# Block-sparse attention with a channel mixer: six sampled block numbers per register load, masked by VectorE, and a new order from the planner

## The chip, the cores and the metric

One Trainium2 chip, one core. The metric is the device time of one execution in microseconds. The kernel before takes 584.38 us, the median of three runs (582.27 to 584.39).

## The reference, cut to what matters

```python
def _attn_ref(q, k, v, sampled_blocks):          # 4 batches, 8 heads, 768 positions, 64 wide
    block, n_blocks = 32, 24
    scores = q @ k^T / sqrt(64)
    mask = neighbouring blocks | first or last block, as row or as column
    for qb in range(n_blocks):
        for kb in sampled_blocks[qb]:            # 3 numbers per query block
            mask[rows of qb, columns of kb] = True
    return softmax(where(mask, scores, -1e9)) @ v

def _moe_ref(x, mu_k, mu_r, w_k, w_v, w_r):      # x: heads side by side, 512 wide
    x_prev = x shifted by one position
    xk, xr = mu_k * x + (1 - mu_k) * x_prev, mu_r * x + (1 - mu_r) * x_prev
    v = relu(xk @ w_k) ** 2 @ w_v                # 512 -> 1024 -> 512
    return sigmoid(xr @ w_r) * v
```

The mixer's weights come as 64-bit numbers, and the kernel converts them. The numbers in `sampled_blocks` are known only at run time.

## The kernel before, in words

The four batches are worked in two pairs (`pr`), 0 and 1. Attention is cut into units. Two wide units, one per pair, hold the first and the last query block, which see all keys. The other 22 query blocks of a pair make 11 near units of two neighbouring query blocks each (`UNITS`, `load_near`, `near_unit`), so there are 22 near units in all. A near unit needs its queries (`q`), eight key blocks for each of its query blocks and the values that belong to them.

Keys lie in one buffer, `KR0`; one load (`kd`) brings the neighbouring blocks and six fetches (`kt`, line 520) bring the sampled ones, three per query block. Since `KR_BUFS` is 1, the keys of a unit can be loaded only when the scores of the unit before are done. Values lie in six buffers `VR`, used in pairs: for each query block one load (`vn`, line 533) and three fetches of sampled blocks (`vt`, line 540).

From the seventh unit on (`CARRY`) the probabilities `p` are transposed in blocks by VectorE (`tb`, line 607), and SyncE moves the pieces back to `p` with four transfers (line 613); the products with the values (line 664) wait for these. The earlier units transpose on TensorE (line 584).

Nearly all transfers are issued by SyncE, from one queue, in the order in which the program has them. A sampled fetch needs a register that holds the block's number. VectorE packs the three numbers of a query block into one word (`pack`, lines 327 to 332). `sampled_block` loads that word into a register, once per query block (a load, a check of its bounds), and then takes a number out of it with a shift and a mask, which are register operations on SyncE ahead of each fetch. The registers of the first pair of batches are used again for the second.

When a batch pair has a tile of 128 positions finished, the mixer works on it: `gate` (`r`, line 862), `hidden` (`h`, line 888 or 904) and `values` (`v`, line 922). Its matmuls stand between those of the attention units, and the last four tiles, taken two at a time, stand at the end.

The order of all operations is set by a planner (`Plan.order`): each operation is added with an engine, a duration, a rank and the buffers it uses, and the planner simulates the engines and places them. The ranks come from tables of numbers (`UNIT_AT`, `KEYS_AT`, `VALUES_AT`, `TILE_AT`, `WEIGHT_AT`, `CONVERT_AT`). The durations that SyncE's operations are planned with are constants: 450 ns for an issue and for each of the four moves of `p`, 680 for a sampled fetch, 640 for the loads of a query block's word. They set the order only; what an operation takes on the chip doesn't depend on them.

Of the kernel before, what the change touches and what calls it, by code (L numbers as in the profile page):

```python
# [9 lines left out]
F32 = mybir.dt.float32  # L10
# [261 lines left out]
def block_sparse_attention_channel_mix(  # L272
# [15 lines left out]
    def fixed(shape, dtype, name):  # L288
        return Fixed(cp.tile(shape, dtype, name=name))
# [13 lines left out]
    packed = fixed([1, NB], I32, "packed")  # L303
# [10 lines left out]
    def mask_setup():  # L314
# [3 lines left out]
        word = buf([P, 2 * NB], F32, "x1", 1, "word")  # L318
# [178 lines left out]
    def load_near(pr, m, i):  # L497
# [27 lines left out]
        for j in range(PAIR):  # L525
# [9 lines left out]
            def gather(w=w, j=j, more=more):  # L535
# [3 lines left out]
                for i in range(NRAND):  # L539
                    nc.sync.dma_start(to[:, i], vt[bass.ds(sampled_block(n + j, i) + pr * NB, 1)].rearrange("o k b x -> (o k) (b x)"))  # L540
# [3 lines left out]
            plan.add(SP, NRAND * FETCH + ISSUE * more, values_at + 0.01 * j, gather, reads=[(packed,)],  # L544
# [59 lines left out]
    def carry(p, keys, name, rank):  # L604
# [10 lines left out]
        plan.add(SP, QB * ISSUE, rank + 0.05, away, reads=[(turned,), (p, *keys)], writes=[(p, *keys)], size=QB * wire(180000, 1024), parts=QB)  # L615
# [416 lines left out]
ISSUE, FETCH, FIND = 450, 680, 640  # L1032
# [20 lines left out]
TWICE = -83.1032  # L1053
# [4 lines left out]
O_MAX, O_EXP, O_TR, O_PV, O_END = 5.0819, 5.7451, 5.4616, 26.0916, 5.9388  # L1058
W_MAX, W_EXP, W_TR, W_PV = -123.0937, 6.5274, 5.6492, -188.6436
O_MIX, O_SQ, O_SQ1 = -0.0059, 100.3872, -9.1324  # L1060
NEAR, STAY, STORE = 78.2721, -9.6694, 0.0
SECOND = 0.4468
UNIT_AT = [
    -10.1623, 39.0943, 41.5342, 48.1709, 60.9108, 87.2056, 142.7255, 143.5689, 209.2752,
    223.9713, 253.2747, 259.3255, 264.4496, 276.0797, 315.2623, 326.072, 346.1908, 362.7343,
    379.7602, 404.9611, 414.6551, 432.6396, 446.0631, 552.0929, 566.7713,
]
KEYS_AT = [
    -10.1028, -44.6072, 30.887, -99.6782, 55.0175, 65.6048, 75.2198, 80.1323, 92.2395,
    97.8406, 117.16, 69.934, 137.2921, 148.3066, 186.9807, 192.5333, 262.4631, 209.2797,  # L1070
    315.8413, 265.1049, 367.6119, 371.1823, 392.2787, 340.6908,
]
VALUES_AT = [
    14.772, -16.2249, 42.8975, 81.9301, -30.9551, 104.2473, 116.8682, -135.6146, 80.6142,
    175.7208, 188.4774, 102.1683, 198.1179, 228.8766, -7.598, -553.0218, -325.0968, -355.2257,
    -606.1065, -400.3997, -436.2148, -1.5444, 196.7775, 208.1251,
]
# [14 lines left out]
T_RATE = 1.5576
# [58 lines left out]
```

## Time and profile before

| | us |
|---|---|
| median of three runs | 584.38 |
| profiled execution, its own time | 583.11 |
| its span, first to last instruction | 581.3 |
| TensorE (PE) busy in the span | 524.7 |
| VectorE (DVE), ScalarE (ACT), GpSimd (POOL) busy | 301.3, 289.5, 298.1 |

Busy times are sums over the instructions of an engine, so idle time is the span less the busy time. The mean granted TensorE clock was 0.977 of full speed. SyncE's instructions are not counted as busy time; what it did is read from the timeline of its queue (SPq). A time in the trace is counted from the span's start.

### The profile page before, as it was taken

What the parts mean: (1) busy time and instruction counts of PE and PEld (TensorE: products, weight loads), DVE (VectorE), ACT (ScalarE), POOL (GpSimd) and SP (SyncE); (2) the same over time, 40 slices, a digit from 0 to 9 for tenths busy, and PEclk for the clock granted to TensorE, in tenths of its full rate; (3) what the DMA queues carried; (4) which work ended last, traced back from release to release, by engine and by line L of the source; (5) the groups of instructions that cost most, each with busy time, mean ns of one, the idle gap of its engine ahead of it and who ended that gap; (6) DMA issues with size and microseconds to landing.
All of it is one profiled execution on the core that took longest, in us unless ns stands there. A gap on an engine that the chain in (4) does not pass through costs nothing.

```text
span 581.3 us, 17991 instructions
## 1 busy us (share of the span) xinstructions
PE 524.7 (90%) x6883; PEld 413.0 (71%) x6883; DVE 301.3 (52%) x787; ACT 289.5 (50%) x707; POOL 298.1 (51%) x368
## 2 busy tenths in 40 slices
PE   7877756899987999799999998987999999999997
PEld 3535434687766778489788876775788788888886
DVE  2587797859954454625554644653565542231201
ACT  3665675548634444715547447355457363514420
POOL 0144548668644607417655257146548269656820
PEclk9999797999998999899999999998999999999999
DMA  8999998888777888977748788866878750010001
GB/s 309 379 359 347 326 329 282 270 290 304 233 226 225 248 266 246 273 237 216 222 126 262 229 266 238 271 180 214 248 224 263 229 136 1 1 54 19 1 19 54
DMA packets 72376, 125.29 MB, mean 216 GB/s; under 512 B 11553, under 2 KB 47010, under 8 KB 72290
## 3 DMA queue, kind: packets, MB, share of 16 engines
q1 hardware_dynamic: 72002, 123.75, 66.9%
q8 instruction: 54, 0.88, 0.6%
q10 hardware_dynamic: 288, 0.39, 0.2%
q14 instruction: 32, 0.26, 0.1%
HBM read 100.77 MB, written 6.55 MB: 185 GB/s over the span
## 4 chain that ended last, share of the span: by engine, by line
PE 56%; DMA 18%; SPq 11%; ACT 5%; issue 4%; DVE 4%; POOL 1%; DVEq 0%; ACTq 0%; POOLq 0%
PE v L922 18%; PE s L628 5%; DMA p<-tb 5%; PE o L664 5%; DMA k_ring<-kw 4%; SPq L540 4%; PE r_1p L862 3%; PE r_0p L862 3%; PE h_1p L888 3%; ACT p L573 3%; DMA KR<-kt 2%; DMA VR<-vt 2%; SPq L520 2%; SPq L613 2%; PE h_3p L888 2%
## 5 line engine op out<-in xcount | busy, mean ns | idle before, releaser
L922 PE MATMUL v<-wv,k 128*128 128x512 f32 (+1 forms) x600 | 141.2, 389 | 0.7 <-ACT z L869 0.7
L922 PEld LDWEIGHTS v<-wv,k 128*128 128x128 f32 x600 | 108.2, 189 | 27.3 <-issue 2.9
L564 DVE CUSTOM_DVE_ANT_1 p<-s,near_mask 128x256 f32<-128x256 f32 x176 | 91.1, 628 | 56.7 <-PE s L628 28.5
L573 ACT ACTIVATE p<-p,nm 128x256 f32<-128x256 f32 x176 | 87.6, 499 | 65.7 <-DVE nm L564 58.3
L628 PE MATMUL s<-KR,q 64*32 64x256 f32 x1408 | 52.3, 412 | 11.2 <-DMA KR<-kt 8.0
L607 DVE STREAM_TRANSPOSE tb<-p 128x1024 f32<-128x1024 f32 x32 | 39.8, 1243 | 29.1 <-DMA p<-tb 23.8
L838 POOL TENSOR_TENSOR xr<-xr_1f,xr 128x256 fp32r<-128x256 f32 x24 | 18.2, 758 | 63.3 <-ACT xr L836 63.0
L628 PEld LDWEIGHTS s<-KR,q 64*32 64x32 f32 x1408 | 27.8, 113 | 28.5 <-issue 13.2
L930 DVE SCALAR_TENSOR_TENSOR z<-v,z 128x512 f32<-128x512 f32 (+1 forms) x25 | 16.7, 668 | 57.7 <-PE v L922 41.4
L664 PE MATMUL o<-VR,p 128*32 128x64 f32 x2048 | 36.6, 220 | 8.4 <-DMA p<-tb 5.4
L664 PEld LDWEIGHTS o<-VR,p 128*32 128x32 f32 x2048 | 31.4, 110 | 15.3 <-DMA p<-tb 8.2
L829 DVE SCALAR_TENSOR_TENSOR xr_0f<-xr_0d,mk,xt 128x128 f32<-128x128 f32 x48 | 20.5, 468 | 33.3 <-POOL xr L838 23.7
L825 POOL TENSOR_TENSOR xr_1d<-xt 128x128 f32<-128x128 f32 x48 | 19.3, 420 | 29.1 <-DVE xr_0f L829 17.3
L573 ACT ACTIVATION_READ_ACCUMULATOR p<-p,nm 128x1 f32 x176 | 33.0, 187 | 0.0
L862 PE MATMUL r_1p<-wr,xr 128*128 128x512 f32 x120 | 30.4, 400 | 0.9 <-ACT h_3k L874 0.9
L862 PE MATMUL r_0p<-wr,xr 128*128 128x512 f32 x120 | 31.2, 402 | 0.0
L417 POOL TENSOR_TENSOR wf<-wf,early 128x512 f32<-128x512 f32 x8 | 10.4, 1295 | 40.4 <-DVE wf L406 31.2
L829 DVE SCALAR_TENSOR_TENSOR xr_1f<-xr_1d,mk,xt 128x128 f32<-128x128 f32 x48 | 17.9, 413 | 22.6 <-POOL xr L838 19.8
L888 PE MATMUL h_1p<-mixed,wk 128*128 128x256 f32 x192 | 26.3, 293 | 3.2 <-issue 3.2
L825 POOL TENSOR_TENSOR xr_0d<-xt 128x128 f32<-128x128 f32 x48 | 20.2, 441 | 16.8 <-DVE xr_0f L829 7.2
L564 DVE DVE_READ_ACCUMULATOR2_ANT nm<- 128x1 f32 x176 | 28.0, 159 | 0.0
L888 PEld LDWEIGHTS h_1p<-mixed,wk 128*128 128x128 f32 x192 | 25.0, 200 | 4.1 <-issue 3.3
(172 smaller groups left out, 1035.8 us busy)
## 6 DMA issues: line engine op xcount, KB each, us to landing
VR<-vn SPq DMA_DIRECT2D x44, 512.0 KB, 4.8
VR<-vt SPq DMA_DIRECT2D x138, 128.0 KB, 3.7
KR<-kt SPq DMA_DIRECT2D x132, 128.0 KB, 3.6
p<-tb SPq DMA_DIRECT2D x128, 128.0 KB, 2.8
KR<-kd SPq DMA_DIRECT2D x22, 512.0 KB, 5.0
v_ring<-vw SPq DMA_DIRECT2D x16, 384.0 KB, 6.0
out<-z SPq DMA_DIRECT2D x23, 256.0 KB, 2.8
q<-qn SPq DMA_DIRECT2D x22, 256.0 KB, 3.8
```

What stands on the lines that cost most here:

```text
L540: nc.sync.dma_start(to[:, i], vt[bass.ds(sampled_block(n + j, i) + pr * NB, 1)].rearrange("o k b x -> (o k) (b x)"))
L564: nc.vector.tensor_tensor_reduce(out=dealt(p.ap[:, cs]), in0=cut(view()), in1=by, scale=-SCALE, scalar=3e38 if first is None else nm.ap[:, ...
L573: plan.add(ACT, 378 + 0.83 * (cs.stop - cs.start), rank, lambda: nc.scalar.activation(p.ap[:, cs], p.ap[:, cs], AF.Exp, bias=nm.ap[:, col ...
L607: plan.add(DVE, 1250, rank, lambda: nc.vector.transpose(out=turned.ap.rearrange("p (k y c) -> p k y c", k=QB, c=BLK), in_=p.ap.rearrange(" ...
L628: nc.tensor.matmul(s.ap[ROWS[j], row, a * 256 : (a + 1) * 256].rearrange("p (x g a) -> p g a x" if carried else "p (x a g) -> p g a x", g= ...
L664: nc.tensor.matmul(o.ap[ROWS[j], h * D : (h + 1) * D], held[gi][1](i, g, j), VR[values[j % PAIR][g]].ap[:, j // PAIR, h * D : (h + 1) * D] ...
L825: sub.tensor_tensor(out=part(d.ap), in0=x.ap[:, two, c, 1 : 1 + TT], in1=x.ap[:, two, c, 0:TT], op=ALU.subtract)
L829: nc.vector.scalar_tensor_tensor(out=part(f.ap[:, i, :]), in0=part(d.ap), scalar=mk.ap[:, which, c : c + 1], in1=x.ap[:, two, c, 0:TT], op ...
L838: plan.add(POOL, 80 + 2.4 * MIX * tw, rank + O_MIX, lambda f=f, cs=cs: nc.gpsimd.tensor_tensor(out=dst.ap[:, 1, cs], in0=f.ap, in1=dst.ap[ ...
L862: nc.tensor.matmul(pr.ap[:, 0:512], xr.ap[:, a, c, :], wr.ap[:, w, c, :], start=(c == 0 and m == 0), stop=(c == CC - 1 and m == 2))
L888: nc.tensor.matmul(ph.ap[:, ff * PAIR * TT : (ff + 1) * PAIR * TT], wk.ap[:, w, c, f * P : (f + 1) * P], xk.ap[:, a, c, :], start=(c == 0 ...
L922: nc.tensor.matmul(pv.ap[:, 0:width], hid[f][2](a), wv.ap[:, w, f, cs], start=(f == 0 and m == 0), stop=(f == FC - 1 and m == 2))
```

## The change

The word is no longer packed. VectorE masks all 72 numbers with one operation to their five low bits, and `packed` holds 72 numbers. SyncE loads the six numbers of a near unit with one load into six registers, without a check of bounds, once for each unit of both pairs; no shift and no mask stands ahead of a fetch. The planner is given other durations for SyncE's operations, and all its tables are new.

```diff
-    packed = fixed([1, NB], I32, "packed")
+    packed = fixed([1, NB * NRAND], I32, "packed")
...
         def pack():
-            v = nc.vector
-            n = number.ap.rearrange("o (a i b) -> o a i b", i=NRAND, b=2)
-            w = word.ap[0:1, 0:NB]
-            v.tensor_copy(out=w, in_=n[:, :, NRAND - 1, 0])
-            for i in range(NRAND - 2, -1, -1):
-                x = word.ap[0:1, NB : 2 * NB]
-                v.tensor_copy(out=x, in_=n[:, :, i, 0])
-                v.scalar_tensor_tensor(out=w, in0=w, scalar=float(ROOM), in1=x, op0=ALU.mult, op1=ALU.add)
-            v.tensor_copy(out=packed.ap, in_=w)
-
-        plan.add(DVE, 1070, -15, pack, reads=[(number,)], writes=[(word,), (packed,)])
+            nc.vector.tensor_single_scalar(out=packed.ap, in_=number.ap.rearrange("o (a b) -> o a b", b=2)[:, :, 0],
+                                           scalar=ROOM - 1, op=ALU.bitwise_and)
+
+        plan.add(DVE, 260, -15, pack, reads=[(number,)], writes=[(packed,)])
...
-    def sampled_block(n, j):
-
-        if n not in sampled:
-            sampled[n] = nc.sync.value_load(packed.ap[0:1, n : n + 1], min_val=0, max_val=ROOM**NRAND - 1)
-        return (sampled[n] >> (5 * j)) & (ROOM - 1)
+    def sampled_block(pr, m, i):
+
+        if (pr, m) not in sampled:
+            n = PAIR * m + 1
+            _, sampled[pr, m] = nc.values_load_multi_w_load_instructions(
+                packed.ap[0:1, n * NRAND : (n + PAIR) * NRAND], engines=[nc.sync.engine], min_val=0, max_val=ROOM - 1,
+                skip_runtime_bounds_check_because="VectorE keeps only the five low bits of each number, and kt and vt have that many blocks")
+        return sampled[pr, m][i]
...
-                                      kt[bass.ds(sampled_block(n + j, i) + pr * NB, 1)].rearrange("o p x -> p (o x)"))
-
-            plan.add(SP, NRAND * FETCH + FIND * (pr == 0) + ISSUE * more, keys_at + 0.01 * j, fetch, reads=[(packed,)],
+                                      kt[bass.ds(sampled_block(pr, m, j * NRAND + i) + pr * NB, 1)].rearrange("o p x -> p (o x)"))
+
+            plan.add(SP, NRAND * FETCH + FIND * (j == 0) + ISSUE * more, keys_at + 0.01 * j, fetch, reads=[(packed,)],
...
-            plan.add(SP, NRAND * FETCH + ISSUE * more, values_at + 0.01 * j, gather, reads=[(packed,)],
+            plan.add(SP, NRAND * FETCH_V + ISSUE * more, values_at + 0.01 * j, gather, reads=[(packed,)],
...
-        plan.add(SP, QB * ISSUE, rank + 0.05, away, reads=[(turned,), (p, *keys)], writes=[(p, *keys)], size=QB * wire(180000, 1024), parts=QB)
+        plan.add(SP, QB * MOVE, rank + 0.05, away, reads=[(turned,), (p, *keys)], writes=[(p, *keys)], size=QB * wire(180000, 1024), parts=QB)
...
-ISSUE, FETCH, FIND = 450, 680, 640
+ISSUE, FETCH, FETCH_V, FIND, MOVE = 470, 560, 720, 330, 690
...
-TWICE = -83.1032
+TWICE = -55.3945
...
-    -10.1028, -44.6072, 30.887, -99.6782, 55.0175, 65.6048, 75.2198, 80.1323, 92.2395,
+    -9.7536, -46.9726, 21.8304, -127.1393, 61.7167, 83.778, 92.0419, 66.861, 102.4082,
...
```

The last pair of lines is the first line of `KEYS_AT`; the other tables and the ranks beside them are changed in the same way. Counted over the program, the transfers stay the same in number (577 issued by SyncE) and size, and TensorE's matmuls in number. TensorE takes the units in the same order between the same tiles of the mixer; pieces of a tile are cut or stand a place earlier or later.

SyncE's program, the keys of the first near unit (KR is the key buffer, kd and kt are the neighbouring and the sampled blocks; an ISA row is a fused address operation or, twice behind a load, the check). Before:

```order
L509 DMA KR_69<-kd 128x1024
L517 DMA KR_69<-kt 128x2x256
L460 TENSOR_LOAD packed
L460 ISA x2
L520 REGISTER_ALU
L520 ISA
L520 DMA KR_69<-kt 128x256
L520 REGISTER_ALU x2
L520 ISA
L520 DMA KR_69<-kt 128x256
```

Now:

```order
L504 DMA KR_69<-kd 128x1024
L512 DMA KR_69<-kt 128x2x256
L453 TENSOR_LOAD packed
L515 ISA
L515 DMA KR_69<-kt 128x256
L515 ISA
L515 DMA KR_69<-kt 128x256
L515 ISA
L515 DMA KR_69<-kt 128x256
L512 DMA KR_69<-kt 128x2x256
```

The shifts and masks and the check are gone. Before, the second group of three fetches had a load of its own and stood behind two wide values, a q and a weight; now it follows the first group without a load.

SyncE's program, the keys of the near unit that is number 5 of the second pair, whose queries are q_5. Before:

```order
L509 DMA KR_69<-kd 128x1024
L520 REGISTER_ALU
L520 ISA
L520 DMA KR_69<-kt 128x256
L520 REGISTER_ALU x2
L520 ISA
L520 DMA KR_69<-kt 128x256
```

Now, the keys of unit 4 of that pair, which stand there with the same rows as those of every unit:

```order
L504 DMA KR_69<-kd 128x1024
L453 TENSOR_LOAD packed
L515 ISA
L515 DMA KR_69<-kt 128x256
L515 ISA
L515 DMA KR_69<-kt 128x256
```

In the second pair there was no load; now one stands between kd and the first fetch of every unit.

SyncE's first transfers (w_r is a weight, qw and kw are the queries and keys of the first wide unit). Before:

```order
L501 DMA q_1_96<-qn 128x512
L469 DMA qw_104<-qw 128x128
L483 DMA k_ring<-kw 128x384 x2
L469 DMA qw_104<-qw 128x384
L493 DMA v_ring<-vw 128x768 x2
```

Now:

```order
L376 DMA early<-w_r 128x1024
L496 DMA q_1_104<-qn 128x512
L464 DMA qw_109<-qw 128x128
L478 DMA k_ring<-kw 128x384 x2
L464 DMA qw_109<-qw 128x384
L488 DMA v_ring<-vw 128x768 x2
```

A weight of 512 KB stands ahead of everything. From here to the first kd there were 7 weights and 13 wide values (v_ring) in the queue, and there are 9 and 12 now; up to the second kd all transfers together are 21.5 MB before and 22.5 MB now, counted from the sizes in the order (of 2^20 bytes).

## Rows read from the trace of the kernel before

**Rows 1.** The page, part 1: busy time, share and instructions of each engine.
```profile
PE 524.7 (90%) x6883; PEld 413.0 (71%) x6883; DVE 301.3 (52%) x787; ACT 289.5 (50%) x707; POOL 298.1 (51%) x368
```

**Rows 2.** Busy time by stretch: us, each engine, granted clock, DMA share, GB/s.
```profile
0.00:60.00 60.00, 48.08 (x616) 27.97 (x623) 34.48 (x107) 31.69 (x60) 17.54 (x24) 1.00 0.97 348
60.00:110.00 50.00, 33.64 (x729) 22.77 (x713) 41.63 (x108) 31.64 (x86) 29.04 (x30) 0.83 0.89 301
110.00:240.00 130.00, 117.67 (x1870) 95.56 (x1868) 82.80 (x217) 70.92 (x191) 74.13 (x92) 0.99 0.82 258
...
345.00:470.00 125.00, 115.42 (x1703) 93.57 (x1704) 69.49 (x185) 65.84 (x173) 62.21 (x81) 0.99 0.78 235
470.00:581.30 111.30, 107.95 (x609) 87.97 (x607) 23.00 (x43) 35.97 (x65) 64.54 (x78) 1.00 0.08 27
```

**Rows 3.** TensorE's waits from 60 to 470 us: total, times, longest.
```profile
PE s L628 <- DMA KR<-kt: 7.3, 4, 3.9
PE o L664 <- DMA VR<-vt: 7.2, 6, 2.2
PE o L664 <- DMA p<-tb: 5.4, 8, 1.6
...
PE s L628 <- DMA p<-tb: 2.9, 1, 2.9
```

**Rows 4.** Timelines of SyncE's queue and of TensorE around 397: start, us, instruction.
```profile
391.03 2.15 SPq L540 DMA_DIRECT2D VR<-vt  x3
393.22 0.57 SPq L501 DMA_DIRECT2D q<-qn  x1
393.85 0.42 SPq L509 DMA_DIRECT2D KR<-kd  x1
394.55 3.65 SPq L520 DMA_DIRECT2D KR<-kt  x6
...
400.76 3.99 PE L628 MATMUL s<-KR,q 64*32 64x256 f32 x64 [2.94 <-DMA p<-tb]
```

**Rows 5.** Timeline of TensorE around 90 us; in brackets the idle time before.
```profile
89.94 3.63 PE L628 MATMUL s<-KR,q 64*32 64x256 f32 x60 [3.92 <-DMA KR<-kt]
```

**Rows 6.** Line 613, the moves of p: ns least, median, most; first and last start.
```profile
L613 SPq DMA_DIRECT2D p<-tb x128: 549/584/1815, 160.9 to 472.5; - x128
```

**Rows 7.** Line 520, a key fetch: ns least, median, most.
```profile
L520 SPq ALU_OP  x220: 32/39/51, 44.5 to 447.5; - x110
L520 SPq FUSED_REGOPS  x132: 37/46/56, 44.6 to 447.6; - x132
L520 SPq MOVE KR<-kt x132: 29/29/38, 44.7 to 447.6; - x132
L520 SPq DMA_DIRECT2D KR<-kt x132: 332/338/1312, 44.8 to 447.7; - x132
```

**Rows 8.** Line 540, a value fetch, likewise.
```profile
L540 SPq ALU_OP  x220: 32/37/45, 68.2 to 466.3; - x110
```

**Rows 9.** Line 460, the load of a word and its check, likewise.
```profile
L460 SPq TENSOR_LOAD <-packed x22: 262/272/833, 43.7 to 217.9; - x22
L460 SPq FUSED_REGOPS  x22: 152/157/187, 44.2 to 218.2; - x22
L460 SPq SEQ_ASSERT  x22: 18/18/33, 44.5 to 218.4; - x22
```

**Rows 10.** The tile packed: what writes it.
```profile
L332 DVE CAST packed<-word x1: 167/167/167, 33.6 to 33.6; 1x24 int32<-1x24 f32 x1
```

**Rows 11.** A stretch by windows (as rows 2), and 64 score matmuls in the chain.
```profile
400.60:404.00 3.40, 3.24 (x52) 1.69 (x58) 0.29 (x1) 2.01 (x3) 0.95 (x2) 0.50 0.55 130
...
302.91 1.89 PE s L628 x64
```

**Rows 12.** DMA issues: count, KB each, median us to landing.
```profile
v_ring<-vw SPq DMA_DIRECT2D x16, 384.0 KB, 6.0
...
early<-w_k SPq DMA_DIRECT2D x8, 512.0 KB, 5.7
```

More of the change, by code (lines that the diff above doesn't have):

```diff
@@ L317, in mask_setup @@
         same = buf([P, NM * NRAND * (SEEN + 1)], F32, "mix", 1, "same")
-        word = buf([P, 2 * NB], F32, "x1", 1, "word")
         near = NM * NRAND * 2
@@ L539, in gather @@
                 for i in range(NRAND):
[L540 removed]
+                    nc.sync.dma_start(to[:, i], vt[bass.ds(sampled_block(pr, m, j * NRAND + i) + pr * NB, 1)].rearrange("o k b x -> (o k) (b x)"))
             plan.add(SP, ISSUE, values_at + 0.01 * j, close, writes=[(VR[w[1]], 0, 1)],
                      release=values_at, size=wire(524288, 4096))
[L544 removed]
+            plan.add(SP, NRAND * FETCH_V + ISSUE * more, values_at + 0.01 * j, gather, reads=[(packed,)],
                      writes=[(VR[w[0]], 0, 1)], release=values_at, size=wire(131072, 4096) * (NRAND + more), parts=NRAND + more)
@@ L1051 @@
 HI_POOL = frozenset([0, 1, 2, 3, 4, 6, 7, 8, 11, 12, 13, 15, 16, 17, 18])
-TWICE = -83.1032
+TWICE = -55.3945
 MIX, PAIRED = 2, 2
 DIF_DVE = frozenset()
[L1058 to L1062, printed above, removed]
+O_MAX, O_EXP, O_TR, O_PV, O_END = 5.1827, -1.1618, 5.448, 23.9717, 5.9215
+W_MAX, W_EXP, W_TR, W_PV = -70.0239, -7.0681, 3.8542, -97.7587
@@ L1063 @@
+O_MIX, O_SQ, O_SQ1 = 11.4431, 106.0873, 0.6193
+NEAR, STAY, STORE = 63.3254, -7.5, 0.0
+SECOND = 0.432
 UNIT_AT = [
-    -10.1623, 39.0943, 41.5342, 48.1709, 60.9108, 87.2056, 142.7255, 143.5689, 209.2752,
-    223.9713, 253.2747, 259.3255, 264.4496, 276.0797, 315.2623, 326.072, 346.1908, 362.7343,
-    379.7602, 404.9611, 414.6551, 432.6396, 446.0631, 552.0929, 566.7713,
+    -61.8832, -25.696, 37.5906, 49.9358, 78.1654, 85.5066, 157.6487, 161.212, 275.2454,
+    285.5443, 286.9539, 292.6665, 295.1158, 306.0497, 338.4866, 357.3848, 372.6401, 387.116,
+    402.6876, 433.7349, 449.2341, 458.429, 471.812, 649.3233, 659.78,
@@ L1067 @@
 ]
 KEYS_AT = [
-    -10.1028, -44.6072, 30.887, -99.6782, 55.0175, 65.6048, 75.2198, 80.1323, 92.2395,
-    97.8406, 117.16, 69.934, 137.2921, 148.3066, 186.9807, 192.5333, 262.4631, 209.2797,
-    315.8413, 265.1049, 367.6119, 371.1823, 392.2787, 340.6908,
+    -9.7536, -46.9726, 21.8304, -127.1393, 61.7167, 83.778, 92.0419, 66.861, 102.4082,
+    105.3862, 105.7081, 101.9988, 186.1311, 171.3023, 227.6819, 236.2033, 210.7076, 295.6457,
+    280.4131, 331.7875, 335.1125, 358.007, 360.5464, 396.6448,
@@ L1072 @@
 ]
 VALUES_AT = [
-    14.772, -16.2249, 42.8975, 81.9301, -30.9551, 104.2473, 116.8682, -135.6146, 80.6142,
-    175.7208, 188.4774, 102.1683, 198.1179, 228.8766, -7.598, -553.0218, -325.0968, -355.2257,
-    -606.1065, -400.3997, -436.2148, -1.5444, 196.7775, 208.1251,
+    10.4329, -3.1608, 46.4477, 77.4216, -159.354, -58.4871, -147.0018, -154.5903, 87.9731,
+    6.7614, 185.1241, 94.7577, 214.0024, 187.9166, 243.0338, -632.1711, -182.2237, -263.2192,
+    -753.6318, -506.0984, -537.4304, -52.2543, 398.2023, 354.7759,
@@ L1077 @@
 ]
 TILE_AT = [
-    73.2635, 167.8862, 227.7911, 277.4888, 302.9729, 352.4914, 394.4098, 433.0114, 555.9713,
-    822.0336, 669.3746, 859.3768,
+    77.1345, 115.5264, 180.0003, 299.7739, 344.6776, 377.3345, 424.4068, 461.1655, 643.2547,
+    890.4742, 727.6284, 1311.9243,
 ]
 WEIGHT_AT = [
-    -20.8248, -53.2243, -52.6791, 13.0687, -45.5517, 21.6385, 4.801, 37.1423, 19.7861,
-    43.5324, 12.8773, 50.241, -13.5655, -74.8683, 54.4146, 116.3902, 92.3941, 67.0115,
-    107.6012, -38.0923,
+    -27.2618, -196.6668, -51.9485, 15.3507, -40.3812, -51.8549, -17.8282, 29.3717, 28.9919,
@@ L1086 @@
+    53.7455, 14.505, 29.6841, -6.6704, -96.8087, 57.9516, 84.1339, 95.247, 98.3682,
+    112.1338, 44.728,
 ]
 CONVERT_AT = [
-    -150.3153, -81.7926, -164.2279, -22.1667, -20.6773, 9.2581, -29.1155, 15.5374, 8.9153,
-    17.1985, 47.2794, 52.7703, 49.9036, -14.0758, 56.4673, 158.3134, 65.1365, 73.8086,
-    76.8627, 55.3873,
+    -103.2448, -184.8302, -198.142, -15.9628, -39.8427, -25.0847, -63.2466, 14.035, -4.7952,
+    53.1975, -4.459, 51.7696, 17.2288, -5.5778, 75.1976, 106.9941, 79.1018, 93.7587,
@@ L1091 @@
+    82.6611, 53.8781,
 ]
-T_RATE = 1.5576
+T_RATE = 1.605
 def kernel(**inputs):
```

## The prediction

> **What bounds the kernel now.** I read the page first, then the busy time by stage, then TensorE's waits, then SyncE's queue where those waits end. TensorE has 524.7 us of work in a span of 581.3 [rows 1]. The stages [rows 2] show where the other 56.6 us are: 11.9 in the first 60 us (the two wide units), 16.4 from 60 to 110, 12.3 from 110 to 240, 9.6 from 345 to 470; the other 6.4 lie from 240 to 345 and in the last 111 us, where nothing is loaded any more (DMA share 0.08) and TensorE runs at 97%. That tail cannot gain from faster issue. The first 60 us cannot either: there the DMA engines are full (share 0.97, 348 GB/s).
>
> Between 60 and 470 us the reader should look at what TensorE waits for [rows 3]: keys (KR) 7.3 us in 4 waits, gathered values (VR) 7.2 us in 6, the transposed probabilities that SyncE moves (p<-tb) 5.4 us in 8, and one wait of the scores of 2.9 us that is put down to p<-tb. These 22.8 us all end with a transfer that SyncE issued. Rows 4 show how such a wait comes about: SyncE issues from 391.03 to 398.20 with hardly a hole between the rows; the last of the six key fetches goes out at the end of that run, and TensorE, which had nothing else in order, starts the scores at 400.76 after 2.94 us. (The view names another transfer, which landed about then; by the program the keys of these scores are the six fetches just ahead.) The largest single wait, 3.92 us for keys at 89.94, is of the same kind [rows 5].
>
> How full is the queue? Six key fetches take 3.65 us, so one per 0.66 us; three value fetches take 2.15, so 0.8 each counting the register work before the first [rows 4]; a move of p takes 0.58 and a hole of about 0.04 to 0.06 [rows 6]. 132 x 0.66 + 132 x 0.80 + 128 x 0.63 is 274 us. The 22 loads of a sampled word with its check come to about 13 us (below), and the some 140 other issues of 0.42 to 0.57 us in this stretch (kd, vn, q, out, weights) to about 65. Of 410 us SyncE is occupied about 350, that is 85%, with one in-order queue for everything.
>
> **The register work that goes.** A key fetch is 1.67 ALU operations of 39 ns on average (220 for 132 fetches), a fused address operation of 46, a move of 29 and the DMA of 338 [rows 7]: 0.478 us. The spacing is 0.66, so the 4.67 instructions have 0.18 us of holes between them, 0.039 each. An ALU operation therefore costs 0.039 + 0.039 = 0.078 us on keys, and 0.037 + 0.039 = 0.076 on values [rows 8]. All 440 go: 33.9 us of the queue, 0.13 per fetch.
>
> The check behind each load goes too: a fused operation of 157 ns [rows 9], an assertion of 18 and two holes, 0.25 us x 22 = 5.6 us.
>
> **The load that is added.** Before, 22 loads of one register at 272 ns [rows 9], all in the first pair of batches, whose words are kept in registers for the second. After, 22 loads of six registers: 11 in the first pair instead of 22, and 11 in the second where there were none. No row shows a load of six. Its lower end is that of one, 0.27 us: the same instruction on the same tile, 24 bytes instead of 4. Its upper end is six single loads, 1.63 us. I take 0.4, near the row, since it is one instruction with one wait. Net, the loads then cost 22 x 0.13 = 2.9 us more, and the queue is relieved of 33.9 + 5.6 - 2.9 = 36.6 us, 10% of what occupies it. By unit that is 12 x 0.13 = 1.56 us of fetch work, plus 0.50 for two checks, plus two single loads less one of six (0.14): 2.2 us in the first pair; 1.56 - 0.44 = 1.1 us in the second. At the upper end the relief is 33.9 + 5.6 - 22 x 1.36 = 9.6 us.
>
> The Trainium skill speaks against my value. Its page "Runtime: NRT & Kernel Launch", section "Instruction fetch mechanics", gives about 200 ns for each register, even in bulk; that page means loads from HBM, and no run here shows a load of six. By it, as an estimate, a load costs 1.2 us and the relief would be about 19 us, half of mine.
>
> **VectorE.** Six small operations of about 0.17 us each (the last is in [rows 10]) become one. Some 0.9 us around 33 us: nothing at the end, because the wide stage waits for its transfers (share 0.97); and if the cover were gone, 0.9 us.
>
> **What TensorE gets of it.** 19 waits hold 22.8 us, 1.2 us on average, about one per near unit (22 units). A unit's queue is shorter by 2.2 or 1.1 us. If each wait shrank by the smaller of itself and this relief, roughly 16 us would go (3.9 to 1.7, 2.9 to 1.8, and nearly all of those of about a us). That is the upper end. The lower end is nothing, if something else is just as late. What is late next are the exchanges between engines: TensorE also waits for VectorE and ScalarE around 60 to 110 us, where VectorE is busy 41.6 of 50 us and DMA share is 0.89 [rows 2]; and faster issue puts more transfers in flight on the same DMA engines. I take half: 8 us, of which some 4 fall before 110, and 4 after.
>
> Then the clock. After the wait at 397.8 the granted clock was 0.50 from 400.6 to 404.0 [rows 11], the 1.2 GHz level, and the 64 score matmuls took 3.99 us [rows 4] where the same 64 took 1.89 at full clock [rows 11]: 2.1 us lost behind a wait of 2.9. If half of the waits go, such a stretch goes with an even chance: I count half of it, 1 us.
>
> **The replan.** The order of TensorE's work stays nearly the same from the first near unit to the tail (the same units between the same tiles, a few tiles earlier or later by one piece), so its work is the same and only the waits move. On SyncE two things change that cost. First, weights come earlier. Ahead of the first kd, two weight pieces of 512 KB are added and one wide value piece of 384 KB is put off [rows 12]: 0.63 MB more; ahead of the second kd, 1.0 MB more (22.5 for 21.5). At 348 GB/s that is 1.9 and 3.0 us in which the full DMA engines (rows of the first stage) do other work. The same pieces are gone later, so most of this is given back by 110 us: I count 1 us of loss, with 0 and 4.6 as bounds (4.6 being the 3.0 and the 1.6 us that 512 KB at the head of the program take at that rate). Second, the six fetches of a unit now stand together where other transfers stood between the two groups of three; values of the first near unit are moved ahead of the second unit's keys. That shortens the wait at 89.94 and may lengthen a wait for values; I count it at nothing, because both are the same queue and the sum of issues is unchanged. The planner's new charges cost nothing by themselves: they only choose the order. What it charges now (560 for a key fetch, 690 for a move) is nearer to rows 4 and 6 than 680 and 450 were, less the ALU work.
>
> **Sum.** -8 (waits) - 1 (clock) + 1 (weights ahead) + 0 (VectorE) = -8 us. The profiled execution took 583.11 us, 1.8 beyond its span; less 8 it is 575.1. The median of the three runs is 584.38, 0.2% above that execution; 584.4 - 8 = 576.4. I say 576.
>
> **Rivals.**
> The load pays for each register, so the change hardly does what it says. At 1.63 us the relief is 9.6 us instead of 36.6. In the second pair a unit then loses 1.67 - 1.56 = 0.1 us rather than gaining, and the load stands between kd and the first fetch, on the way of the keys. A quarter of 8 is 2: about 582.4. For it: the page of the skill above. Against it: no row, but one instruction of 272 ns. Chance 0.10.
>
> The stalls go to what is late next. Faster issue finds full DMA engines until 110 us and VectorE behind it; each of the 22.8 us is taken over by the exchange of scores and probabilities. Loss of 1 for the weights, gain of 1 or 2: 583 to 584. For it: VectorE's 83% from 60 to 110; against it: from 110 on VectorE is busy 64% or less and DMA share 0.82 or less. Chance 0.08.
>
> Slower: the weights ahead of the keys. If the first pair's units start 3.0 us later behind the second kd, and the program's first matmuls 1.6 us later behind the weight that is now its first transfer, and the work has no slack left to take this back, 584.4 + 4.6 = 589.0. It decides as soon as the waits shrink by less than 4.6 - 2.9 = 1.7 us, that is by under a tenth. For it: the DMA share of 0.97. Against it: bytes moved ahead leave the stretch from 60 to 110, which is also near full. Chance 0.15.
>
> **How the numbers follow.** 0.67 for the forecast, whose own range is 567 to 581 (upper and lower bounds of the waits, 16 and about 3 us); 0.10 and 0.08 for the two that end near no change; 0.15 for slower. A measurement of this kernel tells about 0.5% from no change, 2.9 us: faster is below 581.5, slower above 587.3. So faster 0.67, same 0.18, slower 0.15. The range 569 to 587 leaves out some 0.06 below and 0.13 above.
>
> **What would show it.** In the profile after: the fetch lines without ALU operations and key fetches 0.53 us apart; the load of six, whose duration settles the first rival; TensorE's waits for KR, VR and p down from 22.8 to about 12 us; one stretch at the low clock fewer; the first near scores not later than before by more than 2 us. The prediction is wrong if those waits are as long as before, or if they shrink and waits for VectorE and ScalarE grow by as much.

## The result and the profile after

The changed kernel takes 566.5 us, the median of four runs (563.88 to 568.01), where the kernel before took 583.82 beside it (582.27 to 584.39). The ratio is 0.9703, with an interval of 0.966 to 0.9745: 17.3 us faster, where 8 were forecast, and below the range. The profiled execution took 568.01 us with a span of 566.2.

TensorE on the page, and its work by stage (columns as in [rows 2]; the last stages are cut where the attention now ends):

```profile
PE 522.5 (92%) x6883; PEld 417.1 (74%) x6883; DVE 301.9 (53%) x782; ACT 288.9 (51%) x707; POOL 298.6 (53%) x368
```

```profile
0.00:60.00 60.00, 47.24 (x511) 29.00 (x512) 35.71 (x100) 32.34 (x61) 20.70 (x26) 0.86 0.95 339
60.00:110.00 50.00, 36.43 (x692) 23.70 (x690) 40.45 (x108) 29.96 (x85) 26.02 (x26) 0.83 0.93 316
110.00:240.00 130.00, 121.21 (x2062) 99.38 (x2062) 83.53 (x219) 74.38 (x195) 74.52 (x93) 0.99 0.81 256
...
345.00:455.00 110.00, 108.52 (x1626) 89.83 (x1625) 62.60 (x168) 62.09 (x162) 58.92 (x76) 1.00 0.81 246
```

Busy time is 2.2 us less than in [rows 1], idle time 43.7 instead of 56.6. Idle time by stage: 12.8 in the first 60 us (11.9 before), 13.6 from 60 to 110 (16.4), 8.8 from 110 to 240 (12.3), and 1.5 from 345 to 455, where [rows 2] has 9.6 from 345 to 470.

TensorE's waits from 60 to 455 us, the view of [rows 3]:

```profile
PE o L659 <- DMA VR<-vt: 6.1, 3, 3.5
PE t L579 <- ACT p L568: 5.3, 5, 2.1
PE tx L722 <- DVE x L725: 4.1, 4, 1.2
PE h_2p L883 <- DVE z L925: 2.2, 1, 2.2
PE s L623 <- DMA KR<-kt: 1.6, 4, 0.5
```

The waits for KR, VR and p, 22.8 us before, are 7.7; none for p is left. In another profile of the changed kernel (e9) they are 9.6, with 0.3 for p. SyncE's instructions by line, as in [rows 6 to 9] (line 515 fetches keys, 453 is the load, 608 moves p):

```profile
L515 SPq FUSED_REGOPS  x132: 37/46/51, 47.7 to 432.4; - x132
L515 SPq MOVE KR<-kt x132: 29/29/38, 47.8 to 432.4; - x132
L515 SPq DMA_DIRECT2D KR<-kt x132: 327/333/1460, 47.9 to 432.5; - x132
L453 SPq TENSOR_LOAD <-packed x22: 1262/1276/1756, 46.2 to 428.1; - x22
L608 SPq DMA_DIRECT2D p<-tb x128: 543/584/1885, 162.4 to 457.1; - x128
```

The shifts, the masks and the check are gone. The load of six takes 1.276 us, not the 0.4 that I took: the queue is relieved of 33.9 + 5.6 - 22 x (1.276 - 0.272) = 17.4 us, not of 36.6.

Where the time went is seen best between fixed points of the work: the first score matmul of the first near unit, of the second pair, and of that pair's unit 7. Windows of the kernel before, then of the changed kernel, cut at these points:

```profile
56.80:240.20 183.40, 153.85 (x2635) 119.73 (x2636) 125.41 (x325) 102.76 (x278) 106.43 (x124) 0.94 0.84 271
240.20:400.80 160.60, 149.88 (x2050) 125.08 (x2052) 79.15 (x204) 82.22 (x205) 79.74 (x103) 0.99 0.76 230
400.80:581.30 180.50, 175.39 (x1636) 141.53 (x1636) 63.04 (x154) 72.88 (x166) 97.45 (x123) 0.99 0.35 105
```

```profile
62.90:237.20 174.30, 152.35 (x2636) 119.21 (x2632) 119.96 (x319) 99.10 (x270) 99.13 (x118) 0.94 0.84 270
237.20:385.20 148.00, 143.77 (x2033) 122.60 (x2034) 77.81 (x202) 79.21 (x201) 73.82 (x97) 0.99 0.81 251
385.20:566.20 181.00, 176.22 (x1655) 143.82 (x1654) 65.61 (x156) 75.62 (x171) 103.93 (x129) 1.00 0.36 108
```

The near units start 6.1 us later. Up to there TensorE does the same matmuls in both kernels, 567 (the count of the second row takes in the first of the scores). Before, then after:

```profile
0.00:56.80 56.80, 45.58 (x567) 26.64 (x567) 33.70 (x105) 31.69 (x60) 14.48 (x21) 1.00 0.98 349
```

```profile
0.00:62.90 62.90, 50.14 (x568) 31.43 (x568) 38.52 (x107) 34.95 (x67) 21.74 (x27) 0.86 0.95 341
```

TensorE is busy 4.6 us longer with them, at a granted clock of 0.86 instead of 1.00, and idle 1.5 us longer. The keys are not what these scores wait for. SyncE issues the last of the first unit's key fetches by 51.8 us, 1.8 earlier than before, and TensorE goes from the wide unit to the scores without idle time. SyncE's last three key fetches before and after, and these scores after:

```profile
51.86 1.72 SPq L520 DMA_DIRECT2D KR<-kt  x3
```

```profile
50.36 1.46 SPq L515 DMA_DIRECT2D KR<-kt  x3
62.90 1.09 PE L623 MATMUL s<-KR,q 64*32 64x256 f32 x32
```

The first pair takes 9.1 us less, with the same number of matmuls. From the second pair to its unit 7 it is 12.6 less: 6.5 of idle time (10.7 to 4.2) and 6.1 of busy time. TensorE's groups in this stretch that tell most, before and then after (r and h belong to the mixer, o are the value products of attention; behind the count stand busy us and mean ns, then idle us before and what ended it):

```profile
L664 PE MATMUL o<-VR,p 128*32 128x64 f32 x896 | 16.6, 220 | 4.9 <-DMA p<-tb 4.1 <-DMA VR<-vt 0.6
L862 PE MATMUL r_1p<-wr,xr 128*128 128x512 f32 x48 | 12.3, 401 | 0.0
L888 PE MATMUL h_3p<-mixed,wk 128*128 128x256 f32 x96 | 12.1, 280 | 0.0
```

```profile
L659 PE MATMUL o<-VR,p 128*32 128x64 f32 x896 | 14.2, 220 | 0.7 <-issue 0.7
L857 PE MATMUL r_1p<-wr,xr 128*128 128x512 f32 x43 | 11.1, 402 | 0.0
L883 PE MATMUL h_3p<-mixed,wk 128*128 128x256 f32 x84 | 10.9, 282 | 0.0
```

17 matmuls (5 of r_1p, 12 of h_3p) now stand behind that point; they are 2.4 of the 6.1 us. The other 3.7 are the same matmuls in less busy time, the value products above all (2.4 less), whose mean duration is unchanged: they stand closer together. The rest of the program is as long as before (181.0 for 180.5), though the 17 have come to it; before, it began with the scores at the low clock [rows 11].

### The profile page after: what moved, and what is told of

It is laid out like the page before. It is cut to its first block, busy times and chain, and to the rows that moved or that the text cites. A ratio compares the mean times of both kernels' runs of the same rounds, so it can differ in the third digit from the quotient of the medians.

```text
span 566.2 us, 17505 instructions
## 1 busy us (share of the span) xinstructions
PE 522.5 (92%) x6883; PEld 417.1 (74%) x6883; DVE 301.9 (53%) x782; ACT 288.9 (51%) x707; POOL 298.6 (53%) x368
## 4 chain that ended last, share of the span: by engine, by line
PE 62%; DMA 11%; SPq 10%; DVE 8%; issue 4%; ACT 3%; POOL 1%; DVEq 0%; POOLq 0%; ACTq 0%
PE v L917 19%; PE s L623 5%; PE o L659 5%; PE r_0p L857 4%; PE h_2p L883 3%; PE r_1p L857 3%; SPq L535 3%; DMA KR<-kt 3%; SPq L515 3%; PE h_3p L883 3%; DMA p<-tb 2%; DVE p L559 2%; PE h_0p L883 2%; PE h_1p L883 2%; DMA VR<-vt 2%
## 5 line engine op out<-in xcount | busy, mean ns | idle before, releaser
L917 PE MATMUL v<-wv,k 128*128 128x512 f32 (+1 forms) x600 | 139.5, 385 | 1.0 <-ACT z L864 1.0
L623 PE MATMUL s<-KR,q 64*32 64x256 f32 x1408 | 50.7, 391 | 3.0 <-DMA KR<-kt 1.6
L659 PEld LDWEIGHTS o<-VR,p 128*32 128x32 f32 x2048 | 29.7, 110 | 5.6 <-issue 3.4
L659 PE MATMUL o<-VR,p 128*32 128x64 f32 x2048 | 32.6, 220 | 0.7 <-issue 0.7
L820 POOL TENSOR_TENSOR xr_1d<-xt 128x128 f32<-128x128 f32 x48 | 19.3, 422 | 24.5 <-DVE xr_1f L824 12.8
L883 PE MATMUL h_2p<-mixed,wk 128*128 128x256 f32 x192 | 28.1, 307 | 3.9 <-DVE z L925 2.2
L883 PEld LDWEIGHTS h_2p<-mixed,wk 128*128 128x128 f32 x192 | 26.2, 211 | 5.7 <-DVE z L925 2.4
L824 DVE SCALAR_TENSOR_TENSOR xr_0f<-xr_0d,mk,xt 128x128 f32<-128x128 f32 x48 | 17.0, 393 | 24.1 <-POOL xr L833 16.8
L737 ACT COPY xt<-tx 128x512 f32<-128x512 f32 (+2 forms) x32 | 13.6, 458 | 27.8 <-PE tx L722 27.7
```

What stands on the lines that cost most here:

```text
L623: nc.tensor.matmul(s.ap[ROWS[j], row, a * 256 : (a + 1) * 256].rearrange("p (x g a) -> p g a x" if carried else "p (x a g) -> p g a x", g= ...
L659: nc.tensor.matmul(o.ap[ROWS[j], h * D : (h + 1) * D], held[gi][1](i, g, j), VR[values[j % PAIR][g]].ap[:, j // PAIR, h * D : (h + 1) * D] ...
L820: sub.tensor_tensor(out=part(d.ap), in0=x.ap[:, two, c, 1 : 1 + TT], in1=x.ap[:, two, c, 0:TT], op=ALU.subtract)
L824: nc.vector.scalar_tensor_tensor(out=part(f.ap[:, i, :]), in0=part(d.ap), scalar=mk.ap[:, which, c : c + 1], in1=x.ap[:, two, c, 0:TT], op ...
L883: nc.tensor.matmul(ph.ap[:, ff * PAIR * TT : (ff + 1) * PAIR * TT], wk.ap[:, w, c, f * P : (f + 1) * P], xk.ap[:, a, c, :], start=(c == 0 ...
L917: nc.tensor.matmul(pv.ap[:, 0:width], hid[f][2](a), wv.ap[:, w, f, cs], start=(f == 0 and m == 0), stop=(f == FC - 1 and m == 2))
```

## The experiments

All ratios are against the kernel before on the same chip; a us is worked out as a share of 583.8. The same four stretches of the profiled runs, in us, are used throughout (the last one ends with the last value matmul of the mixer):

| run | start of near units | first pair | second pair to unit 7 | rest | ratio |
|---|---|---|---|---|---|
| before | 56.8 | 183.4 | 160.6 | 177.2 | 1 |
| changed / again (e9) | 62.9 / 62.0 | 174.3 / 170.8 | 147.9 / 147.7 | 177.8 / 178.3 | 0.9703 / 0.9711 |
| e1, old order, new loads | 60.7 | 175.2 | 159.3 | 177.6 | 0.9855 |
| e12, e1's program again | 58.1 | 181.1 | 157.7 | 176.8 | 0.9945 |
| e13, old order, operations back | 55.5 | 182.2 | 169.9 | 184.2 | 1.0203 |
| e2, new order, old loads | 62.2 | 179.1 | 148.0 | 179.3 | 0.9801 |
| e14, new order, operations back | 62.2 | 180.0 | 154.4 | 182.3 | 1.0009 |
| e17, more loads, first pair | 62.1 | 180.3 | 149.0 | 177.7 | 0.9882 |
| e18, more loads, second pair | 61.6 | 172.4 | 151.7 | 180.0 | 0.9861 |
| e7, seven units kept | 61.8 | 171.3 | 146.1 | 175.5 | 0.9612 |

### The two halves of the change: e1, e2, e9

e1 has the new loads with the charges and tables of before, so that every engine's order is the old one; e2 has the new order with packed words, shifts and checks. e9 is the changed kernel again.

```diff
 e1, to the changed kernel
-ISSUE, FETCH, FETCH_V, FIND, MOVE = 470, 560, 720, 330, 690
+ISSUE, FETCH, FIND = 450, 680, 640
 ... and all tables and ranks of before
 e2, to the changed kernel
-        return sampled[pr, m][i]
+        return (sampled[n] >> (5 * j)) & (ROOM - 1)
 ... and pack() and the single load of before
```

> The order of before, word for word, with the six-register load, the one mask on VectorE and no shifts. The load takes 1.276 us in the profile of the changed kernel, so SyncE's queue is relieved of 33.9 + 5.6 - 22 x (1.276 - 0.272) = 17.4 us, 5% of what fills it. If the register work is the cause, this alone brings most of the 17 us: 567 to 571. If the new order is the cause, it brings 1 to 4 us: 580 to 583.

> The order of the changed kernel, word for word, with the packed words, one load and check per query block, and the shifts and masks on SyncE. If the register work is the cause, the gain is lost: 580 to 585. If the new order is the cause, most of it stays: 567 to 572, with about 4 us of TensorE's waits for keys and values back.

> The changed kernel itself, so that the three runs beside it stand on the same chip: 0.970 by its first measurement, with an interval of half a per cent to either side.

e1: 0.9855 (0.9798 to 0.9912). e2: 0.9801 (0.9746 to 0.9855). e9: 0.9711 (0.9656 to 0.9766). Each half makes the kernel faster, and the product of e1 and e2, 0.966, is at the lower end of the intervals of the whole (with e12 below, which is e1 again, it is 0.975). The order alone is worth about 11.6 us (8 to 15). In the table, e2 has the whole of the changed kernel's gain between the second pair and its unit 7 (148.0), and e1 hardly any of it (159.3). Up to the second pair e2 has gained nothing (241.3 us, where the kernel before is at 240.2). TensorE's waits for KR, VR and p divide in the same way. In e2, where SyncE does all the old register work, they fall from 22.8 us to 12.6; in e1, in the old order, to 17.9. Those of e2, then of e1:

```profile
PE o L664 <- DMA VR<-vt: 7.2, 4, 2.8
...
PE s L628 <- DMA KR<-kt: 3.6, 5, 1.5
...
PE o L664 <- DMA p<-tb: 1.8, 4, 0.6
```

```profile
PE o L660 <- DMA VR<-vt: 6.2, 5, 1.8
PE s L624 <- DMA KR<-kt: 5.7, 3, 3.5
...
PE o L660 <- DMA p<-tb: 3.3, 7, 1.3
...
PE s L624 <- DMA p<-tb: 2.7, 1, 2.7
```

### Loads meant to be done twice: e4, e12

```diff
+            nc.values_load_multi_w_load_instructions(... same six numbers ..., "the values are not used")
             _, sampled[pr, m] = nc.values_load_multi_w_load_instructions(
```

> The changed kernel with each six-register load done twice; 22 x 1.28 = 28 us more in SyncE's queue, and nothing else. If TensorE still hangs on SyncE's queue, a third or a half of it shows: 575 to 581. If after the replan the queue is covered, under 3 us: 566 to 569.

> The old order with the new loads (as e1), each load done twice: 28 us more for SyncE than e1, about 11 us more than the kernel before. In the new order the same doubling brought 3 to 4 us (e4). If the new order is faster because its queue has more slack, the old order pays more: by e1, where 17.4 us of relief gave 8 us, 28 us cost 13, and the ratio is about 1.005. If both orders have the same slack it pays 3 to 4 us: 0.992.

The rows of the loads, of e4 and of e12, show 22 loads and not 44: nothing reads the added load's registers, and it is not in the trace. (In e17 and e18, below, the added loads are read, and there the traces have 33.)

```profile
L456 SPq TENSOR_LOAD <-packed x22: 1262/1283/1601, 45.0 to 425.8; - x22
```

```profile
L457 SPq TENSOR_LOAD <-packed x22: 1264/1280/1678, 43.6 to 439.4; - x22
```

So e4 (0.9758, 0.9699 to 0.9816) is the changed kernel a third time, and e12 (0.9945, 0.9904 to 0.9987) is e1 a second time, but for 22 semaphore instructions of 17 ns where the added loads stood. The doubled loads say nothing of the price of the queue, and where later expectations reckon with "e4's 3 to 4 us" or with e12, that figure has no ground. What they give is the spread: e1's program gained 8.5 us on one chip and 3.2 on another. They differ in the place too: the first pair is 8.2 us shorter than before in e1 and 2.3 in e12.

### The price of a load: e8

```diff
+            for h in range(PAIR):      # two loads of three registers instead of one of six
```

> The changed kernel with each load of six split in two loads of three, 44 instead of 22. If the price is one register's 0.27 us and 0.2 for each further register, a load of three takes 0.67 us, the queue gets 1.5 us more over the program, and the ratio stays 0.970. If more than one register costs 1 us whatever the number, a load of three takes 1.2 to 1.3 us, the queue gets 25 us more, and by e4 the ratio is about 0.975.

```profile
L455 SPq TENSOR_LOAD <-packed x44: 662/678/966, 45.7 to 432.8; - x44
```

One register takes 0.272 us [rows 9], three 0.678, six 1.276: 0.20 for each register beyond the first ((0.678 - 0.272) / 2 = 0.203, (1.276 - 0.272) / 5 = 0.201). The ratio was 0.9778 (0.973 to 0.9826), 4 us over the changed kernel; the 1.5 us that the loads add to the queue do not account for that, and the intervals touch.

### The price of the queue: e13, e14, e17, e18, e7

e13 (on e1) and e14 (on the changed kernel) put 440 register operations back ahead of the fetches, as many as before; the values stay the same. e17 and e18 load the six numbers a second time ahead of the value fetches, in one pair each, and the value fetches use these registers. e7 keeps the registers of the first pair's last seven units for the second pair: 15 loads instead of 22.

```diff
 e13, e14
-        return sampled[pr, m][i]
+        x = sampled[pr, m][i]
+        return (x & (ROOM - 1)) if i % NRAND == 0 else ((x & 63) & (ROOM - 1))
 e17 (e18: pr == 1); use is 1 where a value fetch asks, 0 where a key fetch does
+        use = use * (pr == 0)
+        if (pr, m, use) not in sampled:
 ...
 e7
+        pr = 0 if m >= NM - KEEP else pr      # KEEP = 7
         if (pr, m) not in sampled:
```

> The old order with the new loads (as e1), with the 440 register operations put back ahead of the fetches as before (one ahead of the first of three, two ahead of the others; the values stay the same): 33.9 us more for SyncE than e1, 0.13 per fetch. If the spacing of the fetches is what e1 gained by, the gain is gone: 0.998 to 1.005. If the queue's length at the price that the doubled load showed (5 us for 28) is all, 6 us: 0.996. If the check, the place of the loads or VectorE's pack brought it, it stays near 0.99 or below.

> The changed kernel with the 440 register operations put back ahead of the fetches. By the doubled load in the new order (3 us for 28) 4 us: 0.977. If the spacing counts, it comes to e2 (new order, old loads, 0.980) or above: 0.980 to 0.985.

> The changed kernel with a second load of the same six numbers ahead of the value fetches of each unit of the first pair (the values then use these registers): 11 loads of 1.28 us, 14 us more of SyncE's queue, all in the first pair. If a us of the queue costs the same everywhere (17 us for 33.9, e14), 7 us: 0.983. If the second pair pays most of it (e7: 5 us for 9), 3 us: 0.976.

> The same in the second pair alone: 14 us more of SyncE's queue there. If a us of the queue costs the same everywhere, 7 us: 0.983, and the first pair ends as in the changed kernel. If the second pair pays most of it, 8 to 11 us: 0.985 to 0.990.

> The changed kernel, with the six registers of the last seven units of the first pair kept for the second: 15 loads of six instead of 22, about 9 us less for SyncE, all of it in the second pair. From e4 (28 us more of loads cost 3 to 4 us) 9 us less would bring about 1 us: ratio 0.968. If each load stands on the path of its unit's keys, 1.28 us go for each of seven units: 0.955. If the second pair's queue is covered (TensorE idle for 1.5 us only from 345 to 455), nothing: 0.970.

e13: 1.0203 (1.016 to 1.0246). e14: 1.0009 (0.9978 to 1.0041). e17: 0.9882 (0.9834 to 0.9929). e18: 0.9861 (0.9822 to 0.99). e7: 0.9612 (0.9562 to 0.9663). Against 0.971 for the changed kernel and 0.990 for e1's program (the middle of its two results), 33.9 us more in the queue cost 17 us in the new order and 18 in the old one; 14 us more cost 10 in the first pair and 9 in the second; 9 us less brought 6. By these five runs a us of SyncE's queue is worth 0.5 to 0.7 us, in both orders and both pairs. Each cost is uncertain by some 3 us, which is 0.1 for 33.9 us of queue and 0.2 to 0.4 for 14 or 9. The change's own relief of 17.4 us came out lower: 8.5 and 3.2 us in the old order (e1's program) and 5 in the new one (e2 to the changed kernel), that is 0.2 to 0.5. Whether relief is worth less than added work costs, or this is the spread, is open. The windows of e17 and e18, cut as above, show the cost where the loads were put:

```profile
62.10:242.40 180.30, 155.36 (x2636) 120.37 (x2632) 120.05 (x319) 99.25 (x270) 99.39 (x118) 0.92 0.85 263
242.40:391.40 149.00, 144.37 (x2033) 122.87 (x2032) 77.93 (x202) 78.79 (x201) 73.28 (x96) 0.99 0.81 247
```

```profile
61.60:234.00 172.40, 152.89 (x2632) 118.91 (x2632) 119.52 (x320) 98.75 (x270) 98.97 (x117) 0.94 0.87 274
234.00:385.70 151.70, 144.38 (x2031) 122.91 (x2030) 77.73 (x202) 80.11 (x202) 74.12 (x97) 0.99 0.81 244
```

With e17 the first pair is as long as in e14 (180.3 and 180.0) and the second as in the changed kernel; with e18 it is the other way round. e7, whose saved loads are all in the second pair, is the fastest version that was run.

### The place of the load: e10, e11

```diff
-        plan.add(SP, ISSUE, keys_at, lambda: nc.sync.dma_start(... kd ...),
+        plan.add(SP, ISSUE, keys_at, lambda: (sampled_block(pr, m, 0), nc.sync.dma_start(... kd ...)),
```

> The changed kernel with each load of six issued just ahead of kd, the first transfer of the unit's keys, instead of behind it; the rest of the order stays. The load then runs while kd waits for the key buffer to come free, and the first key fetch is issued 1.28 us sooner behind kd. If the load costs through the path of the keys (TensorE's 1.6 us of waits for KR, and the starts of units), up to 1.28 us times some units go: 0.965. If it costs only as length of the queue, its place is worth nothing: 0.970, and the waits for KR stay at 1.6 us.

> Both: seven units' registers kept and the 15 loads issued ahead of kd. e7 gave 0.961. If place and number are both worth something, 0.957; if only the length of the queue counts, 0.961 as in e7.

e10: 0.9738 (0.9681 to 0.9795). e11: 0.9674 (0.9619 to 0.9728). The place brings nothing that can be seen: beside e9 the waits for KR are longer (e9's row, then e10's), and e11 gains 4 us over e10, where e7 gains 6 over e9.

```profile
PE s L623 <- DMA KR<-kt: 4.1, 7, 1.0
```

```profile
PE s L623 <- DMA KR<-kt: 7.5, 7, 2.2
```

### What the new order consists of: e3, e6, e15, e16

```diff
 e3, kernel before         ISSUE, FETCH, FETCH_V, FIND, MOVE = 470, 680, 800, 640, 690 (before: 450, 680, 680, 640, 450)
 e6, changed kernel        ... = 450, 680, 680, 640, 450
 e15, changed kernel       ... = 470, 560, 720, 330, 450
 e16, changed kernel       ... = 470, 680, 680, 640, 690 (changed: 470, 560, 720, 330, 690)
```

> Before, with its loads and its tables, but the planner charges SyncE's operations as the profile of before shows them with the old register work: 470 for an issue, 680 for a key fetch, 800 for a value fetch, 690 for a move of p. If it is enough that the planner knows what a move costs, 570 to 577. If the gain needs tables that were sought anew under these charges, 580 or more; it may even be slower than before, since the old tables were sought under the old charges.

> The changed kernel with the planner's charges of before (issue 450, fetch 680 for keys and values, find 640, move 450) and the new tables: with e3 it is the fourth corner of charges and tables. If the tables alone bring the order's gain of about 2 per cent, the ratio stays at 0.970 to 0.975. If charges and tables only fit together, as e3 (1.012) suggests, it comes to 0.98 or more, and TensorE's waits for KR, VR and p grow from 7.7 us towards the 22.8 of before.

> The changed kernel with the planner's charge of a move of p at 450, as before, instead of 690; the other charges and the tables stay, and the plan is made anew. If this charge is what keeps TensorE from waiting for p (8.3 us before, none in the changed kernel), those waits come back and the ratio is 0.980 to 0.985. If charges and tables only fit as a whole, it is 0.985 or more, by waits of other kinds. If neither, 0.971.

> The changed kernel with the planner's charges of the fetches as before (680 for keys and values, 640 for the load) instead of 560, 720 and 330; a move of p stays at 690. If the fetches' charges are the part that matters, waits for KR and VR come back: 0.985 to 1.005. If the moves' charge is it, 0.971 to 0.975.

e3: 1.0116 (1.0069 to 1.0163). e6: 1.0091 (1.0059 to 1.0123). e15: 0.9958 (0.9934 to 0.9983). e16: 1.0026 (0.9995 to 1.0058). Each is a plan of its own: e6, e15 and e16 are 14 to 22 us slower than the changed kernel, and e3 is 7 us slower than the kernel before. The waits of e15, in which only the moves of p are charged as before:

```profile
PE tx L722 <- DVE x L725: 6.3, 5, 3.5
...
PE tx L722 <- ACT h_1k L869: 3.2, 1, 3.2
PE o L659 <- DMA p<-tb: 3.2, 5, 1.2
PE h_2p L883 <- ACT h_1k L869: 3.1, 3, 2.6
```

The waits for p do come back, but with 3.2 us they are a part of the 14 us; more is lost to exchanges with VectorE and ScalarE. In these four runs charges and tables fit only together.

### Weights later: e5

Three weights are moved back on SyncE in the changed kernel: the first w_r to where the kernel before had it, one w_v and one w_k behind the first near unit's key fetches. The other engines keep their order.

```diff
 ... (ops is the planner's order, w the loads of the weights in it)
+        for op, behind in ((w[0], w[1]), (w[4], keys_of_first[-1]), (w[7], keys_of_first[-1])):
+            ops.remove(op)
+            ops.insert(ops.index(behind) + 1, op)
```

> The changed kernel with nothing moved but three weights on SyncE: the first w_r goes back to where it stood before, and one w_v and one w_k piece (512 KB each) go behind the first near unit's key fetches; every other engine's order is that of the changed kernel. If my rival's mechanism (weights ahead of the keys delay the near units) costs the changed kernel something at the end, the first near scores come 2 to 3 us earlier than in the changed kernel and the ratio falls from 0.970 to about 0.965. If weights ahead are lent and given back (the theory that I now hold), the first near scores come earlier, but the end does not: 0.970 to 0.976. If the early weights are themselves what makes the new order faster, it is slower than 0.976.

e5: 0.9782 (0.9729 to 0.9835). The near units start at 67.4 us, later and not earlier. ScalarE's timeline and a wait of TensorE in e5 show why:

```profile
59.03 0.66 ACT L396 ACTIVATE wmag<-raw 128x512 f32<-128x512 f32 x1 [6.36 <-DMA raw<-w_v]
```

```profile
PE o_-1_535 L716 <- ACT ptw L596: 4.5, 1, 4.5
```

ScalarE, in its own order, waits 6.36 us for the weight that was put off, and the probabilities of the wide unit (ptw) wait behind it. So e5 doesn't price the early weights: their conversions would have to move with them. That was not tried.

## Why the prediction was wrong

**The load, mis-sized.** I took 0.4 us; it measured 1.276. The rival that it pays for each register was right in kind, though its 1.63 us was too high: a register beyond the first costs 0.20, not 0.27. The page "Runtime: NRT & Kernel Launch" of the Trainium skill, section "Instruction fetch mechanics", gives about 0.2 us for each register, told there of loads from HBM. This load from an on-chip tile agrees with it (0.20, e8), and the estimate of 19 us of relief that I made from it stood against 17.4 by the measured load. The rival's time, 582.4, did not come.

**The worth of the queue.** Half of an upper end of 16 us for 36.6 us of relief is 0.22 us for each us. The runs that added or took away work show 0.5 to 0.7 (e14, e13, e17, e18, e7), the change's own relief 0.2 to 0.5 (e1's program 8.5 and 3.2 us, e2 to the changed kernel 5). So 0.22 was at the low end of what was measured, or under it. By my own price 17.4 us would have given 4; that -8 stands near the upper of these results is luck, a relief taken twice too large at a price that was rather too low. I had reckoned that a wait can fall no further than its own length and that half of that would be late elsewhere. A reason that fits the higher price, but that no run parts from others, is that SyncE is one in-order queue, 85% occupied by my own estimate, so that what stands in it late is late for the units that follow.

**The replan, the step that failed.** "The order of TensorE's work stays nearly the same ..., so its work is the same and only the waits move", and of SyncE's new order "I count it at nothing, because both are the same queue and the sum of issues is unchanged". This was counted at nothing, with +1 for the weights. The order is worth -11.6 us by itself (e2), the larger part of the 17.3, and about 11 again from e1's program to the changed kernel and from e13 to e14. That waits would move was right; that moving them without fewer issues gains nothing was wrong. With the old register work and the new order, TensorE's waits for KR, VR and p are 10.2 us shorter (e2, 22.8 to 12.6), with the new loads and the old order 4.9 (e1). The gain lies between the second pair and its unit 7: 12.6 us in e2 as in the changed kernel, where TensorE stands idle 4.2 us instead of 10.7 and has 17 matmuls less to do, and where the same matmuls stand closer. The scores that waited 2.94 us at 400.76 [rows 4] do not wait now. Which of the moved pieces or transfers brings this was not tested and stays open.

**The planner's charges "cost nothing by themselves".** They only choose the order, but that choice moves the time by +7 to +22 us when either half is changed alone (e3, e6). What of the new order's gain comes from truer charges, and what from a longer search of tables under any charges, stays open: tables found for one set of charges did not work with the other, so no run here parts the two.

**Rival "slower".** Weights ahead of the keys were to delay the near units. The first kd is indeed issued 2.8 us later (45.20 for 42.41; I gave 1.9), and the near units start 6.1 us later (62.9 for 56.8), between 61.6 and 62.9 in the runs of the new order in the table, where the old order started between 55.5 and 60.7. But the mechanism was another: these scores did not wait for keys. The wide unit's work lasts until they start, and 4.6 of the 6.1 us are the same matmuls in a stretch with a lower granted clock. In the old order, too, this work is longer where the clock is lower (busy for 46.0 us at 0.97 in e13, 48.8 at 0.89 in e1). The order's own part shows in TensorE's idle time up to there: 12.8 to 14.4 us in the runs of the new order in the table, 9.5 to 11.8 in those of the old. Whether the early weights make this part stays open: e5, which moves three of them back, starts later still. The sequel was wrong as well, since the first pair takes the delay back (174.3 for 183.4).

**The clock.** One stretch at 1.2 GHz fewer was counted with -1. The rows of the granted clock over 40 slices, before and after, show rather more of them in the first 100 us:

```profile
PEclk9999797999998999899999999998999999999999
```

```profile
PEclk9987878898999999999999998999999999999999
```

The stretch at 400 us [rows 11] is gone, but the mean over the span is 0.963 after 0.977. In the first 60 us it is 0.86 where [rows 2] has 1.00, and 0.91 in e9. It varies between executions of one program (e9: 0.973 over the span), so the term of -1 is neither shown nor refuted.

**VectorE.** The new operation was not measured apart; what it changes is inside e1.

**What the list of signs said.** Key fetches 0.54 us apart instead of 0.66: right (three in 1.42 us, the last of them 0.33, so two spacings in 1.09), by SyncE's timeline of the changed kernel:

```profile
373.33 1.42 SPq L515 DMA_DIRECT2D KR<-kt  x3
```

Waits from 22.8 to 12: it was 7.7. Waits for other engines did not grow by as much. The first near scores later by no more than 2 us: wrong, 6.1.

## What to carry to other kernels

Before a us of an in-order queue is priced by the waits that it ends, ask how full the queue is, and put work into it or take work out to see: here, at 85% by an estimate, a us of issue came to 0.5 to 0.7 us of the whole in such runs, and the change's own relief to 0.2 to 0.5. The order in a queue can be worth more than its length: the same issues in another order took 10 us off TensorE's waits. A new order from a planner is a change of its own, to be bounded from both sides (here -2% for the whole new order, +1% for the new charges with the old tables, and +4% against the changed kernel for the old charges with the new tables) and to be run apart from the code that comes with it. A register load of several numbers is to be priced by the number, and numbers that are used again are worth keeping in registers (e7, 6 us beyond the changed kernel).

## What was not expected of the hardware

SyncE's load from an on-chip tile takes 0.272 us for one register, 0.678 for three and 1.276 for six. A load whose registers nothing reads did not reach the chip at all (22 loads in e4 and e12, 33 in e17 and e18). Two measurements of one program, on different chips, gave 0.9855 and 0.9945; half a per cent to either side is to be reckoned with beside the intervals.
